# The turn of y in halves of 64 columns, moved behind the state's update

## The chip, the cores and the metric

The kernel runs on one core of a Trainium2 chip. The metric is the time of one execution on the device in microseconds (us); the kernel's figure is the median of several runs. Matrix products run on TensorE (PE; its weight loads are PEld), elementwise work on VectorE (DVE), ScalarE (ACT) and GpSimd (POOL), and SyncE (SP) issues most DMA transfers. Each engine works through its own queue in order; semaphores tie the queues together.

## The reference

Linear attention with a decaying state feeds a layer of eight experts, of which each token uses two. The part that matters here is the attention, with 4 batches, 8 heads, 768 positions and a head width of 64:

```python
for t in range(S):
    state = gamma[None, :, None, None] * state + np.einsum('bhd,bhe->bhde', k[:, :, t], v[:, :, t])
    y[:, :, t] = scale * np.einsum('bhd,bhde->bhe', q[:, :, t], state)
...
x = np.ascontiguousarray(attn_out.transpose(0, 2, 1, 3)).reshape(B * S, H * D)
logits = x @ w_gate
noise_scale = np.log1p(np.exp(x @ w_noise))
noisy_logits = logits + noise_scale * noise
```

The two largest noisy logits of a token choose its experts; each expert is `relu(x @ w1) @ w2`, weighted and added.

## The kernel before, in words

The attention is done in 24 chunks of 128 positions (six per batch; j counts them, c = j % 6). One pass of the loop `for j in range(NCH)` (L822) holds these stages of TensorE:

- **qk(j + 1)** (L353): scores of the next chunk, keys against scaled queries. VectorE masks them into `am` (L356, two instructions).
- **the turn of chunk j - 1**, `x_turn` (L401): y lies as heads by positions and is multiplied, as the stationary operand of 128 columns, with a table `turn` of 144 columns (an identity and the gate's weights), so that it comes out as positions by channels with the logits beside it. Behind it the **squares' sums** (L405): four products of `sq`, the squares of y, with a column of ones.
- **y_state(j)** (L368): queries against the state U that the chunk found (none where c = 0).
- `middle`: products for the lists of tokens that only some chunks have: route_p (L492, L494) in chunks 15 and 23, own_m (L582) in chunk 18.
- **y_mm(j)** (L375): masked scores against scaled values, added to y_state's result. ScalarE copies the result to `yt` (L379).
- **pU(j)** (L384): keys against values, added to the state (none where c = 5). ScalarE copies it to `U` (L386), then squares y into `sq` (L388).

All of a chunk's other work is issued between y_state and y_mm: GpSimd scales values (`v_scale`, L326) and queries (`q_scale`, L334) ahead of time; VectorE computes a token's scale (`x_scale`, L420, L421) from the squares' sums, ScalarE writes the high half of the turned x (x16, L427) and copies the logits (L415), VectorE writes the low half (lo, L431) and SyncE writes both to `xbuf` (L432). `mid` holds VectorE's extra work of single chunks, issued before lo; `todo` stands behind it, and `first_todo` behind y_mm: there ScalarE sums the squares of expert weights (w_sum, L207) and makes their high halves (w_hi, L230). w_hi in chunk 9 needs a scale that a small product (w_scale, L217) yields. The result of the turn, pT, and that of y, pY, have one buffer each, so the next turn waits for lo, and the next y_state for yt.

The order of every queue is the order of the program. The pools decide only how far an engine may run ahead: `vp` has two buffers, `sq` one. From chunk 18 on GpSimd gathers the first expert's tokens, and SyncE transposes them by DMA (`x_t`, L741). Behind the loop TensorE starts on the first expert (L873 to L875) while the last turn and the rest of the lists are done.

Of the kernel before, what the change touches and what calls it, by code (L numbers as in the profile page):

```python
# [20 lines left out]
C = 128  # L21
# [80 lines left out]
def moe_kernel(ctx, tc, qT, kT, kt, vt, noise, wgn, w1, w2, ctab, qtab, xbuf, out):  # L102
# [219 lines left out]

    def v_scale(j):
        c = j % NC
        VP[j] = loads.tile([128, H, D], F32, name="vp", bufs=2)
        nc.gpsimd.tensor_tensor(VP[j], IN["v", j].rearrange("p (h d) -> p h d", h=H),  # L326
                                vtab[:, c, :, None].to_broadcast([128, H, D]), op=OP.mult)

# [18 lines left out]
    def qk(j):  # L347
        AM[j] = loads.tile([128, 2, HP, C], F32, name="am", bufs=2)
        pA = [psum.tile([128, HP, C], F32, name="pA", bufs=2) for _ in range(2)]
        for i in range(HP):  # L350
            for s in range(2):
                r = slice(s * 64, s * 64 + 64)
                nc.tensor.matmul(pA[s][:, i, :], IN["k", j][r, i, :],  # L353
                                 QS[j][r, i, :], start=True, stop=True)
        for s in range(2):
            nc.vector.tensor_tensor(AM[j][:, s], pA[s], mask[:, None, :].to_broadcast([128, HP, C]), op=OP.mult)  # L356
# [5 lines left out]
    def y_state(j):  # L362
        c = j % NC
        PY[j] = loop_psum.tile([128, 2, 512], F32, name="pY")
        for i in range(HP if c else 0):
            for s in range(2):
                r = slice(s * 64, s * 64 + 64)
                nc.tensor.matmul(yplace(j, i, s), U[c % 2][r, i, :], QS[j][r, i, :],  # L368
                                 start=(i < 2), stop=False, skip_group_check=True)

    def y_mm(j):
        c = j % NC
        for i in range(HP):
            for s in range(2):
                nc.tensor.matmul(yplace(j, i, s), VP[j][:, 2 * i + s, :], AM[j][:, s, i, :],  # L375
                                 start=(not c and i < 2), stop=True, skip_group_check=True)
        YT[j] = loads.tile([128, 2, 2, C], F32, name="yt", bufs=2)
        y = YT[j].rearrange("p s g c -> p (s g c)")
        nc.scalar.activation(y.rearrange("p (s x) -> p s x", s=2), PY.pop(j)[:, :, :2 * C], AF.Copy)  # L379
        if c < NC - 1:  # L380
            for i in range(HP):
                for s in range(2):
                    h = 2 * i + s
                    nc.tensor.matmul(pU[s * 64:s * 64 + 64, i, :], IN["kt", j][:, h * 64:h * 64 + 64], VP[j][:, h, :],  # L384
                                     start=(c == 0 and i == 0), stop=True, skip_group_check=True)
            nc.scalar.activation(U[(c + 1) % 2], pU, AF.Copy)  # L386
        SQ[j] = loads.tile([128, KT, C], BF, name="sq", bufs=1)
        nc.scalar.activation(SQ[j].rearrange("p n c -> p (n c)"), y, AF.Square)  # L388

    def x_turn(j):  # L390

        b, c = divmod(j, NC)
        v = int(b >= B0)
        t = loop_psum.tile([128, 2, 512], F32, name="pT").rearrange("p s x -> p (s x)")
        PT[j] = p = t[:, 512 - 2 * XW:512 + 2 * XW]
        p = p.rearrange("p (s x) -> p s x", s=2)
        PT[j, "s"] = t[:, 512 + 2 * XW:513 + 2 * XW]
        y = YT.pop(j)
        for s in range(2):
            for g in range(2):  # L400
                nc.tensor.matmul(p[:, s, g * 128:g * 128 + XW], y[:, s, g, :], turn[:, v, 2 * s + g],  # L401
                                 start=(g == 0), stop=True, skip_group_check=True)
        q = SQ.pop(j)
        for n in range(KT):
            nc.tensor.matmul(PT[j, "s"], q[:, n], oneb[:, 0:1], start=(n == 0), stop=(n == KT - 1), skip_group_check=True)  # L405
        PT[j, "y"] = PT[j].rearrange("p (n x) -> p n x", x=XW)[:, :, :128]
# [343 lines left out]
    def P(j, f, *a, d=mid):  # L750
        d.setdefault(j, []).append((f, a))
# [34 lines left out]
    P(22, route_m, 1)  # L786
    at0(22, route_c, 1)
    P(23, route_p, 1, d=middle)
    P(23, route_n, 1)
    P(23, route_g, 1)  # L790
    at(0, turn_gate, 0)
    at(3, turn_ident, 1)
    at(3, turn_gate, 1)
# [28 lines left out]
    for j in range(NCH):  # L822
        if j + 1 < NCH:
            qk(j + 1)
        if j:
            x_turn(j - 1)
        y_state(j)
        for f, a in middle.get(j, []):
            f(*a)
        if j < 2:  # L830
            q_scale(j + 2)
        if j + 1 < NCH:
            v_scale(j + 1)
        if 2 <= j < NCH - 2:
            q_scale(j + 2)
        if j:
            x_scale(j - 1)
        for f, a in mid.get(j, []):
            f(*a)
        if j < NC - 3:  # L840
            q_table(j + 3)
        if j + AHEAD < NCH:
            load(j + AHEAD)
        if j:
            x_split(j - 1)
        for f, a in todo.get(j, []):
            f(*a)
        y_mm(j)
        for f, a in first_todo.get(j, []):
            f(*a)  # L850
    lctx.close()
# [427 lines left out]
```

## Time and profile before

| | |
|---|---|
| median of 3 runs | 646.7 us (646.54 to 647.61) |
| profiled execution | 645.92 us |
| its span | 644.1 us |
| PE busy | 634.5 us, 99% |
| ACT busy | 300.2 us, 47% |
| DVE busy | 287.6 us, 45% |
| POOL busy | 204.0 us, 32% |

The loop over the chunks ends near 110 us; the experts take the rest. The busy time of PE counts matmuls whose ends are modelled, so stages are best measured from one start to the next. In a row of PE, 128*64 128x128 is the stationary operand (partitions * columns: the tile of the array that is used) and the moving one (partitions x columns); a float32 product makes two records, one for each pass.

### The profile page before, as it was taken

The numbers are of one execution on the slowest core, as the hardware profiler recorded it, in microseconds if no ns is written. First come the engines' busy times: TensorE is split into PE (matmuls) and PEld (weight loads), VectorE is DVE, ScalarE is ACT, GpSimd is POOL, SyncE is SP. The second block draws the span as 40 slices with busy tenths as digits, with TensorE's granted clock in tenths as the row PEclk, the third lists the DMA queues.
The fourth block names the chain that finished last, engine by engine and source line by source line (L and its number), as shares of the span: only waits on it lengthen the run. The fifth ranks groups of instructions, "written<-read, shape, count | busy, mean of one in ns | idle before, by whom it ended". The sixth has DMA issues, their size and how long they took to land.

```text
span 644.1 us, 12255 instructions
## 1 busy us (share of the span) xinstructions
PE 634.5 (99%) x4919; PEld 390.3 (61%) x4919; DVE 287.6 (45%) x740; ACT 300.2 (47%) x559; POOL 204.0 (32%) x166
## 2 busy tenths in 40 slices
PE   9999999999999999999999999999999999999995
PEld 6999998549578544554455445544554465455574
DVE  4678785897454221654162226222622262215020
ACT  6577457615652543554354345434543454344121
POOL 4555472041540134104410433043304430430214
PEclk9999999999999999999999999999999999999999
DMA  8999999978888066845773576447654784483303
GB/s 300 379 386 382 335 319 268 371 188 295 167 139 263 4 130 113 235 99 101 148 191 136 91 137 182 162 82 132 192 161 82 120 211 147 86 118 62 50 10 43
DMA packets 94423, 113.02 MB, mean 175 GB/s; under 512 B 60662, under 2 KB 61820, under 8 KB 90780
## 3 DMA queue, kind: packets, MB, share of 16 engines
q1 hardware_dynamic: 82576, 85.57, 44.2%
q0 software_dynamic: 11776, 26.63, 23.4%
q8 instruction: 40, 0.66, 0.4%
q14 instruction: 19, 0.16, 0.1%
q10 hardware_dynamic: 12, 0.01, 0.0%
HBM read 72.66 MB, written 26.42 MB: 154 GB/s over the span
## 4 chain that ended last, share of the span: by engine, by line
PE 95%; ACT 2%; DVE 1%; issue 1%; POOL 0%; DMA 0%; POOLq 0%; ACTq 0%
PE pH L873 13%; PE pH L875 13%; PE pH L874 13%; PE pO L919 12%; PE pO L921 12%; PE pO L920 12%; PE pA L353 4%; PE pT L401 4%; PE pY L375 4%; PE pT L975 2%; PE pY L368 2%; PE pO L963 2%; PE pU L384 1%; ACT junk L207 1%; PE pO L951 1%; PE pO L949 1%
## 5 line engine op out<-in xcount | busy, mean ns | idle before, releaser
L910 POOL DMA_INDIRECT out<-ot,idx x51 | 82.4, 1616 | 323.2 <-ACT ot L905 181.1
L873 PE MATMUL pH<-xe,w1h 128*128 128x384 f16 (+5 forms) x576 | 180.9, 314 | 0.4 <-DVE hl L882 0.4
L875 PE MATMUL pH<-xe,w1l 128*128 128x384 f16 (+5 forms) x576 | 180.8, 314 | 0.0
L874 PE MATMUL pH<-xe,w1h 128*128 128x384 f16 (+5 forms) x576 | 180.8, 314 | 0.0
L882 DVE SCALAR_TENSOR_TENSOR hl<-pH,hh 128x384 f16<-128x384 f32 (+5 forms) x144 | 75.6, 527 | 140.0 <-ACT hh L879 139.5
L921 PE MATMUL pO<-w2h,hl 128*128 128x512 f16 x344 | 130.4, 379 | 0.0
L920 PE MATMUL pO<-w2l,hh 128*128 128x512 f16 x344 | 130.4, 379 | 0.0
L919 PE MATMUL pO<-w2h,hh 128*128 128x512 f16 x344 | 130.3, 379 | 0.0
L879 ACT ACTIVATE hh<-pH 128x384 f16<-128x384 f32 (+5 forms) x144 | 67.3, 467 | 122.5 <-PE pH L875 111.7
L905 ACT ACTIVATE ot<-pO,gse 128x512 f32<-128x512 f32 x45 | 30.9, 687 | 155.7 <-PE pO L921 139.5
L235 DVE SCALAR_TENSOR_TENSOR w1l<-wst,wsc,w1h 128x1024 f16<-128x1024 f32 x28 | 35.9, 1284 | 95.3 <-ACT w1h L230 95.3
L873 PEld LDWEIGHTS <-w1h 128*128 128x128 f16 x576 | 56.3, 98 | 33.0 <-issue 2.7
L875 PEld LDWEIGHTS <-w1l 128*128 128x128 f16 x576 | 56.3, 98 | 30.9
L874 PEld LDWEIGHTS <-w1h 128*128 128x128 f16 x576 | 56.3, 98 | 30.3 <-issue 0.5
L207 ACT ACTIVATE junk<-wst 128x1024 bf16<-128x1024 f32 x64 | 67.2, 1050 | 0.1
L723 POOL DMA_INDIRECT xg<-xbuf,idx x54 | 57.4, 1062 | 29.0 <-issue 11.9
L921 PEld LDWEIGHTS <-hl 128*128 128x128 f16 x344 | 33.6, 98 | 40.6
L919 PEld LDWEIGHTS <-hh 128*128 128x128 f16 x344 | 33.6, 98 | 40.6 <-issue 0.4
L920 PEld LDWEIGHTS <-hh 128*128 128x128 f16 x344 | 33.6, 98 | 39.6
L356 DVE TENSOR_TENSOR am<-pA,mask 128x512 f32<-128x512 f32 x48 | 30.8, 683 | 17.9 <-PE pA L353 17.9
L326 POOL TENSOR_TENSOR vp<-in_v,cs 128x512 f32<-128x512 f32 x24 | 25.2, 1049 | 36.3 <-issue 16.3
L230 ACT ACTIVATE w2h<-wst,wsc 128x1024 f16<-128x1024 f32 x32 | 36.5, 1140 | 0.2 <-DVE wsc L185 0.2
(181 smaller groups left out, 681.3 us busy)
## 6 DMA issues: line engine op xcount, KB each, us to landing
wst<-w SPq DMA_DIRECT2D x28, 1024.0 KB
in_q<-qT SPq DMA_DIRECT2D x24, 256.0 KB
in_k<-kT SPq DMA_DIRECT2D x24, 256.0 KB
in_v<-vt SPq DMA_DIRECT2D x24, 256.0 KB
in_kt<-kt SPq DMA_DIRECT2D x24, 256.0 KB
xbuf<-x SPq DMA_DIRECT2D x24, 256.0 KB
out<-zero SPq DMA_DIRECT2D x6, 1024.0 KB
wst<-w SPq DMA_DIRECT2D x8, 512.0 KB
```

What stands on the lines that cost most here:

```text
L207: nc.scalar.activation(junk, st[:, i * 1024:(i + 1) * 1024], AF.Square, accum_out=ss[:, i:i + 1])
L230: nc.scalar.activation(hi, st[:, i * 1024:(i + 1) * 1024], AF.Copy, scale=sc[:, 0:1])
L723: nc.gpsimd.indirect_dma_start(out=x[:n], out_offset=None, in_=xbuf[:128 + B0 * S] if e == 0 and t < 3 else xbuf, in_offset=bass.IndirectO ...
L873: nc.tensor.matmul(p[:, :n], whi, xh, start=(k == 0), stop=False)
L874: nc.tensor.matmul(p[:, :n], whi, xl, start=False, stop=False)
L875: nc.tensor.matmul(p[:, :n], wlo, xh, start=False, stop=(k == KT - 1))
L879: nc.scalar.activation(hh[:, f, n0:n1], p, AF.Relu)
L882: nc.vector.scalar_tensor_tensor(hl[:, f, n0:n1], p, 0.0, hh[:, f, n0:n1], op0=OP.max, op1=OP.subtract)
L910: nc.gpsimd.indirect_dma_start(out=out, out_offset=bass.IndirectOffsetOnAxis(ap=idx[:n, i:i + 1], axis=0), in_=ot[:n], in_offset=None, com ...
L919: nc.tensor.matmul(p, a, WT["2h"][:, f, :], start=(f == 0), stop=False)
L920: nc.tensor.matmul(p, a, WT["2l"][:, f, :], start=False, stop=False)
L921: nc.tensor.matmul(p, c, WT["2h"][:, f, :], start=False, stop=(f == FT - 1))
```

## The change

The turn is issued behind y_mm and pU of the chunk, where it stood between qk and y_state. Its four products with 128 stationary columns become eight with 64, each pair writing the two halves of the partitions. y_mm and pU move from the end of the pass to directly behind y_state, ahead of the other engines' work of the pass. `middle` stays behind the turn, and so now stands behind y_mm. `vp` gets a third buffer, `sq` a second. route_n and route_g of the last chunk move from `mid` to `todo`, behind lo.

```diff
-        VP[j] = loads.tile([128, H, D], F32, name="vp", bufs=2)
+        VP[j] = loads.tile([128, H, D], F32, name="vp", bufs=3)
...
-        SQ[j] = loads.tile([128, KT, C], BF, name="sq", bufs=1)
+        SQ[j] = loads.tile([128, KT, C], BF, name="sq", bufs=2)
...
         for s in range(2):
             for g in range(2):
-                nc.tensor.matmul(p[:, s, g * 128:g * 128 + XW], y[:, s, g, :], turn[:, v, 2 * s + g],
-                                 start=(g == 0), stop=True, skip_group_check=True)
+                for r in (slice(0, 64), slice(64, 128)):
+                    nc.tensor.matmul(p[r, s, g * 128:g * 128 + XW], y[:, s, g, r], turn[:, v, 2 * s + g],
+                                     start=(g == 0), stop=True, skip_group_check=True)
...
-    P(23, route_n, 1)
-    P(23, route_g, 1)
+    at(23, route_n, 1)
+    at(23, route_g, 1)
...
         if j + 1 < NCH:
             qk(j + 1)
+        y_state(j)
+        y_mm(j)
         if j:
             x_turn(j - 1)
-        y_state(j)
         for f, a in middle.get(j, []):
...
         for f, a in todo.get(j, []):
             f(*a)
-        y_mm(j)
         for f, a in first_todo.get(j, []):
             f(*a)
```

TensorE's queue in a plain chunk, before, from the end of one turn to the next turn (x8 counts the products; a size is partitions x columns of the result):

```order
L405 MATMUL pT<-oneb,sq 128x1
L368 MATMUL pY<-qs,U_170 64x128 x8
L375 MATMUL pY<-am,vp 64x128 x8
L384 MATMUL pU<-vp,in_kt 64x64 x8
L353 MATMUL pA<-qs,in_k 128x128 x8
L401 MATMUL pT<-turn,yt 128x144 x4
```

The same engine after the change, at a chunk without pU (17), where the new line of the turn is L402 and that of the squares L406:

```order
L406 MATMUL pT<-oneb,sq 128x1
L353 MATMUL pA<-qs,in_k 128x128 x8
L368 MATMUL pY<-qs,U_171 64x128 x8
L375 MATMUL pY<-am,vp 64x128 x8
L402 MATMUL pT<-turn,yt 64x144 x8
L406 LDWEIGHTS sq
```

The turn has moved from behind qk to behind y_mm, and in this chunk nothing stands between the two.

ScalarE's queue around the two w_hi of chunk 9, before (x is x16, lgs the logits, w1h the high half of weights):

```order
L427 ACTIVATE x_926<-pT,xsa 128x512
L415 ACTIVATE lgs_317<-pT 128x32
L379 ACTIVATE yt<-pY 128x512
L386 ACTIVATE U_170<-pU 128x256
L388 ACTIVATE sq<-yt 128x512
L230 ACTIVATE w1h<-wst_474,wsc_476 128x1024 x2
L427 ACTIVATE x_1012<-pT,xsa 128x512
```

And after:

```order
L428 ACTIVATE x_983<-pT,xsa 128x512
L416 ACTIVATE lgs_342<-pT 128x32
L230 ACTIVATE w1h<-wst_507,wsc_509 128x1024 x2
L379 ACTIVATE yt<-pY 128x512
L386 ACTIVATE U_171<-pU 128x256
L388 ACTIVATE sq<-yt 128x512
L428 ACTIVATE x_1073<-pT,xsa 128x512
```

Before, yt and U of chunk 9 stood ahead of the two w_hi; now these stand ahead of yt and U of chunk 10.

## Rows read from the trace of the kernel before

**Rows 1.** Part 4 of the page: chain that ended last, by engine.

```profile
PE 95%; ACT 2%; DVE 1%; issue 1%; POOL 0%; DMA 0%; POOLq 0%; ACTq 0%
```

**Rows 2.** Timeline of PE, one chunk: start us, length us, engine, line, operation, records, [idle before].

```profile
66.43 1.16 PE L353 MATMUL pA<-qs,in_k 64*128 64x128 f32 x16
67.52 1.25 PE L401 MATMUL pT<-turn,yt 128*128 128x144 f32 x8
68.60 0.24 PE L405 MATMUL pT<-oneb,sq 128*128 128x1 bf16 x4
68.78 0.67 PE L368 MATMUL pY<-qs,U 64*64 64x128 f32 x16
69.37 1.09 PE L375 MATMUL pY<-am,vp 128*64 128x128 f32 x16
70.30 0.63 PE L384 MATMUL pU<-vp,in_kt 128*64 128x64 f32 x16
```

**Rows 3.** Timelines of PE cut at stage ends (last records alone), and the last turn.

```profile
70.70 0.23 PE L384 MATMUL pU<-vp,in_kt 128*64 128x64 f32 x2
70.86 0.83 PE L353 MATMUL pA<-qs,in_k 64*128 64x128 f32 x10
...
109.44 0.28 PE L375 MATMUL pY<-am,vp 128*64 128x128 f32 x2
109.65 0.34 PE L873 MATMUL pH<-xe,w1h 128*128 128x384 f16 x1
...
111.61 1.14 PE L401 MATMUL pT<-turn,yt 128*128 128x144 f32 x8
112.59 0.24 PE L405 MATMUL pT<-oneb,sq 128*128 128x1 bf16 x4
```

**Rows 4.** Timelines of PE, DVE and ACT around chunk 9.

```profile
47.39 0.24 PE L405 MATMUL pT<-oneb,sq 128*128 128x1 bf16 x4
...
48.91 0.75 DVE L431 SCALAR_TENSOR_TENSOR x<-pT,xsa,x 128x512 f16<-128x512 f32 x1 [0.89 <-ACT lgs L415]
...
48.10 0.69 ACT L427 ACTIVATE x<-pT,xsa 128x512 f16<-128x512 f32 x1 [0.48 <-DVE xsa L421]
...
50.58 2.18 ACT L230 ACTIVATE w1h<-wst,wsc 128x1024 f16<-128x1024 f32 x2
...
53.85 0.60 ACT L379 ACTIVATE yt<-pY 128x512 f32<-128x512 f32 x1 [0.42 <-PE pY L375]
54.34 0.38 ACT L386 ACTIVATE U<-pU 128x256 f32<-128x256 f32 x1
```

**Rows 5.** Timelines of PE and DVE around chunks 16 and 17.

```profile
78.03 0.24 PE L405 MATMUL pT<-oneb,sq 128*128 128x1 bf16 x4
...
80.28 1.16 PE L353 MATMUL pA<-qs,in_k 64*128 64x128 f32 x16
81.47 1.22 PE L401 MATMUL pT<-turn,yt 128*128 128x144 f32 x8
...
80.58 0.74 DVE L431 SCALAR_TENSOR_TENSOR x<-pT,xsa,x 128x512 f16<-128x512 f32 x1
```

**Rows 6.** Timelines of PE and POOL at chunk 18: own_m and the q scaling behind the gather.

```profile
86.60 0.45 PE L582 MATMUL pR<-ob,a 128*128 128x7 f16 x12
...
90.53 1.27 POOL L334 TENSOR_TENSOR qs<-in_q,gq 128x512 f32<-128x512 f32 x1
```

**Rows 7.** Timelines of PE, SP (issues) and ACT at the loop's end.

```profile
99.50 0.24 PE L405 MATMUL pT<-oneb,sq 128*128 128x1 bf16 x4
...
106.50 1.25 PE L401 MATMUL pT<-turn,yt 128*128 128x144 f32 x8 [0.24 <-ACT yt L379]
...
97.74 0.94 SPq L203 DMA_DIRECT2D wst<-w  x2
...
102.23 2.12 SPq L741 DMA_TRANSPOSE xe<-xg  x1
...
102.86 1.06 ACT L207 ACTIVATE junk<-wst 128x1024 bf16<-128x1024 f32 x1
```

## The prediction

> **What bounds the kernel now.** I read the chain of waits first. TensorE is 95% of the chain that ended last [rows 1], so a change in this loop is worth what it takes off TensorE's own row of work, and costs what it makes TensorE wait. The timeline of one chunk comes next [rows 2]: from one qk to the next are 70.86 - 66.43 = 4.43 us, no row carries an idle mark, and the stages meet end to end. qk takes 1.09 us to the start of the turn, the turn 1.08 to the squares' sums, these 0.18, y_state 0.59, y_mm 0.93 and the pU stage 0.56. So the loop is TensorE-bound in its plain chunks, and its other engines have slack there; the question is where a chunk carries extra work for ScalarE, VectorE or GpSimd, and what that work holds up in the new order.
>
> **The turn itself.** The four products of the turn become eight with half the stationary columns. Two products whose outputs lie in different halves of the partitions run side by side today: eight y_mm products of 64 columns, sixteen passes over 128 moving columns, take 0.93 us [rows 2], and one after the other sixteen passes of the turn's kind would take far more, since eight of them fill the 0.98 us from 111.61 to 112.59 [rows 3]. In y_mm a pair therefore takes 0.93 / 8 = 0.12 us. The turn's moving operand is 144 columns wide, so a pair of half turns should take what one whole pass takes now, 0.98 / 8 = 0.12 us. The halving as such is worth nothing either way; what it does is give the turn the 128*64 shape of y_mm and pU.
>
> **The order of the stages.** A boundary at which the tile's shape changes costs more than a step. From the last pair of pU to the next qk are 70.86 - 70.70 = 0.16 us where a pU step is (70.70 - 70.30) / 7 = 0.06: 0.10 extra. From the last pair of y_mm to a whole-array product are 109.65 - 109.44 = 0.21 us where a step is 0.12: again 0.10 [rows 2, 3]. Entering costs too: the turn of the last chunk, which stands between whole-array products, takes 0.98 us, that of the loop 1.08 [rows 2, 3]. So a chunk of the new order is qk 1.09 (it leaves for another shape, as now) + y_state 0.59 + y_mm 0.93 + pU 0.40 + 0.06 = 0.46 (no change behind it) + turn 0.98 + 0.10 (nothing on entering, 0.10 on leaving) + squares 0.18 = 4.33 us. That is 0.10 less than 4.43. It counts in chunks 1 to 22, so -2.2 us. The bounds are 0 and -0.2 per chunk: no change, or both boundaries of the turn free.
>
> The Trainium skill (TensorEngine Tiling (Array Packing), Key Properties) says that changing the tiling mode, not just the tile, drains TensorE. Rows 3 agree, with some 0.10 us at a change. Counted by that rule alone, both orders have four changes per chunk and the loop gains nothing; the rows say that what is lost on entering also depends on the stage entered. This is a rival below.
>
> **The end of the loop.** In the last chunk the turn of chunk 22 waits 0.24 us for yt [rows 7], because no qk stands before it. In the new order a turn and the squares lie between pU and the next y_state, and y_mm and pU's successor never wait for yt. From pU to the first product of the experts there were five changes of shape (turn, y_state, route_p, y_mm, expert), now three (y_state, y_mm, squares; route_p and the expert follow in the squares' shape). Two changes at 0.10 and the 0.24 make -0.44 us, bounded by -0.24 and -0.7. route_n and route_g now stand behind lo of chunk 22: VectorE work beside TensorE's first expert products, priced at nothing.
>
> **New waits.** GpSimd's and SyncE's queues keep their order. On ScalarE yt, U and sq of a chunk move ahead of x16, of the q tables (chunks 0 to 2; q is scaled more than a chunk before its use, so at nothing) and of what the lists add. The turn stands some 2 us later against qk than before, so what hangs on the turn (x_scale, x16, lo, and what is queued behind them) is late against the next y_state and the next turn. Plain chunks have room. Three places do not; I time each from the start of the squares' sums.
>
> (a) Chunks 9 to 11. ScalarE's two w_hi start 50.58 - 47.39 = 3.19 us after the squares [rows 4]; they wait for a scale whose product now stands directly behind the squares, so 3.0. In the old order yt and U of the chunk stood ahead of them; now yt and U of chunk 10 stand behind. 3.0 + 2.1 for the two and 0.87 from yt's start to U's end (54.34 + 0.38 - 53.85) gives U at 5.97. TensorE wants it for y_state(11) at 0.2 (squares and the scale's product) + 4.33 + 1.09 = 5.6. Wait 0.3. Then x16 of chunk 9 stands behind U and sq: about 6.5, and lo ends 48.91 + 0.75 - 48.10 = 1.56 later, at 8.1. Chunk 11 has no pU, so turn(10) is wanted at 5.9 + 0.59 + 0.93 = 7.45. Wait 0.6. Together +0.9, from 0.3 to 1.3.
>
> (b) Chunk 17 has no pU either. VectorE's list work delays lo of chunk 15, and the turn of 16 starts 81.47 - 78.03 = 3.44 us after the squares [rows 5], 0.15 after lo. It would be ready at 0.18 + 1.09 + 0.59 + 0.93 = 2.79. Wait 0.65, of which today's 81.47 - 80.28 - 1.09 = 0.10 is there already: +0.55, from 0.3 to 0.8.
>
> (c) Chunk 18. own_m now stands behind the squares and directly before qk(20), where y_mm and pU used to follow it. From own_m's start to the end of the q scaling behind the first gather GpSimd needs 90.53 + 1.27 - 86.60 = 5.20 us [rows 6]. qk(21), which reads it, is now wanted after own_m's 0.4 and one chunk, 0.4 + 4.33 = 4.73 after own_m's start. Wait +0.5, from 0 to 0.7. The third vp buffer does not help: the gather stands ahead in GpSimd's queue and waits for own_m's result. The second sq buffer only keeps sq(j) from waiting for the squares of j - 1.
>
> Chunk 3, where VectorE builds the second turn table, is of this kind but not in the sum; it is part of the range's upper side.
>
> (d) SyncE's queue. The last transpose of the first expert's tokens is issued 102.23 - 99.50 = 2.73 us after the squares of chunk 21, behind xbuf's write, which waits for lo. The first expert product stood 109.65 - 102.23 = 7.42 us behind that issue. Now the squares of that turn are followed by 0.18 + 4.33 + (3.39 - 0.44 = 2.95) us of TensorE's work, so 7.46 - 2.73 = 4.73 us are left. Its landing is not shown. The nearest rows: weight pieces issued at 97.74 were read at 102.86, so 5.1 us at most; the transpose's issue alone takes 2.12 us where two weight pieces take 0.94 [rows 7]. I take 5.6, nearest the weight pieces and somewhat above for the longer issue: wait +0.9. The bounds are 2.1 (its issue: no wait) and 7.42 (+2.7).
>
> Sum: -2.2 + 0.9 + 0.55 + 0.5 = -0.25 for the loop, -0.44 + 0.9 = +0.45 for its end, **+0.2 us**. The later stages keep their work; a shift here passes through, TensorE being the chain. The profiled run took 645.92 us (span 644.1), so 646.1 there; against the median of 646.7 it is 646.9.
>
> **Rivals.** *The cover holds* (faster): the engines beside TensorE run far enough ahead at (a) to (c) and the transpose lands in time. Then -2.2 - 0.44 = -2.6, 644.1 us. For it: rows 2 show no idle anywhere. Against: in (a) to (c) the queue orders are fixed and the durations are read. *The transpose lands late* (slower): at 7.42 us after issue the first expert product waits 2.7, the sum is -0.25 - 0.44 + 2.7 = +2.0, 648.7 us; it is slower beyond the bound from a landing of about 6.7 us on. For it: weights and transposes share one queue. Against: nothing waits for it today. *A change of shape costs the same whichever stage is entered* (slower): four per chunk as before, the 2.2 is not there, +2.4, 649.1 us; the skill's rule above read alone. Against: 0.98 and 1.08 for the same turn in rows 2 and 3. *The halves do not run side by side*: 23 turns in the loop and one behind it, eight passes more each, 24 x 0.98 = 23.5, 670 us. Against: y_mm's pairs.
>
> **How the numbers follow.** Forecast 0.56, its own range 645.7 to 648.4; cover holds 0.18; transpose late 0.14; equal cost of changes 0.08; halves in turn 0.04. A measurement of this kernel tells about 0.2%, 1.3 us, from no change. Faster: 0.18 + 0.04 from the forecast's lower end = 0.22. Slower: 0.14 + 0.08 + 0.04 + 0.04 from its upper end = 0.30. Same 0.48. The range 644.9 to 649.1 takes in the forecast, the late transpose, equal changes and the part of the first rival that falls short of its full gain; it leaves out the serial halves and the rest of the first rival, under 0.2.
>
> **What would show it.** In the profile after, a plain chunk of 4.33 us with a turn of 1.08 behind pU shows the step of the shapes; idle before y_state in chunk 11 (released by ScalarE's U), before the turns of 10 and 16 (by VectorE's lo) and before qk(21) (by GpSimd's q scaling) shows (a) to (c); idle before the first expert product, released by a transpose, shows (d). A plain chunk of 4.43 or more, or a turn of 2 us, would make the prediction wrong, and so would a loop without those waits.

## The result

The changed kernel takes 655.04 us (median of 4 runs, 653.75 to 655.19) against 646.62 us: a ratio of 1.0128 [1.0115, 1.0141]. The forecast was 646.9 us with a range of 644.9 to 649.1; the change is slower by 8.4 us and the range misses it by 6. The profiled execution took 653.75 us (span 651.7), 7.8 us more than that of before, so all times of places below add up against 7.8, not 8.4. A ratio in this document is worked out from the runs of both kernels, with its interval, and need not equal the quotient of their medians.

The chain that ended last has lost the single owner that it had in [rows 1]:

```profile
PE 86%; DVE 5%; DMA 4%; ACT 2%; issue 1%; SPq 1%; POOL 0%; POOLq 0%; ACTq 0%; DVEq 0%
```

A plain chunk of the changed kernel, in the timeline of PE (start us, length us, engine, line, operation, records, [idle before]), beside [rows 2]:

```profile
69.11 1.16 PE L353 MATMUL pA<-qs,in_k 64*128 64x128 f32 x16
...
71.72 0.64 PE L384 MATMUL pU<-vp,in_kt 128*64 128x64 f32 x16
72.18 1.15 PE L402 MATMUL pT<-turn,yt 128*64 128x144 f32 x16
73.27 0.25 PE L406 MATMUL pT<-oneb,sq 128*128 128x1 bf16 x4
73.45 0.71 PE L353 MATMUL pA<-qs,in_k 64*128 64x128 f32 x8
```

From qk to qk are 73.45 - 69.11 = 4.34 us, against 4.43 in [rows 2]; pU takes 0.46 and the turn 1.09. That part came as forecast (4.33). What did not are the waits of PE, which the timeline marks in brackets with what ended them:

```profile
58.52 1.20 PE L402 MATMUL pT<-turn,yt 128*64 128x144 f32 x16 [0.66 <-DVE x L432]
...
63.45 1.20 PE L402 MATMUL pT<-turn,yt 128*64 128x144 f32 x16 [0.96 <-DVE x L432]
...
85.98 1.20 PE L402 MATMUL pT<-turn,yt 128*64 128x144 f32 x16 [0.49 <-DVE cum L547]
...
96.76 1.71 PE L353 MATMUL pA<-qs,in_k 64*128 64x128 f32 x16 [0.95 <-POOL qs L334]
...
101.40 1.20 PE L402 MATMUL pT<-turn,yt 128*64 128x144 f32 x16 [0.85 <-DVE x L432]
...
113.26 0.67 PE L368 MATMUL pY<-qs,U 64*64 64x128 f32 x16 [1.79 <-ACT U L386]
...
116.74 0.32 PE L874 MATMUL pH<-xe,w1h 128*128 128x384 f16 x1
116.91 0.32 PE L875 MATMUL pH<-xe,w1h 128*128 128x384 f16 x1
```

The first expert product starts at 116.74 us instead of 109.65 [rows 3]: 7.1 of the 7.8 us are lost by then. (The last turn, now of half tiles between whole-array products, takes 0.35 more; the rest passes through.) I measured each stage against its length in a plain chunk and got these losses:

| place | us more | forecast |
|---|---|---|
| first stages, before any turn | 0.75 | 0 |
| qk(6) behind chunk 3's tables | 0.73 | named, not priced |
| small: chunks 8 and 9 (0.2), y_state(11) (0.16) | 0.4 | 0.3 for y_state(11) |
| turn(10), turn(11) | 0.85 + 1.15 | 0.6 for turn(10) |
| turn(16) | 0.7, of which 0.1 before the change | 0.55 |
| qk(21) | 1.57 | 0.5 |
| turn(19) | 1.05 | 0 |
| y_state(23), turn(22) | 1.86 + 0.58 | 0 |
| first expert product, for the transposes | 0 | 0.9 |

Together 9.6 us, against some 2.5 us gained by the shapes and at the loop's end. The first line is not the change's: the second pass starts at 10.80 before and 11.55 here, but over the profiles of all kernels below it lies anywhere between 10.67 and 11.55, with no regard to the edit.

**What VectorE did there.** In the timelines of DVE and POOL of the changed kernel (two halves of w1l on one row are "x2"):

```profile
55.29 2.42 DVE L242 SCALAR_TENSOR_TENSOR w1l<-wst,wsc,w1h 128x512 f16<-128x512 f32 x2
...
93.10 2.95 DVE L443 TENSOR_TENSOR lg<-lgs 128x96 f32<-128x96 f32 x1
95.98 1.28 DVE L356 TENSOR_TENSOR am<-pA,mask 128x512 f32<-128x512 f32 x2
...
97.42 3.17 DVE L242 SCALAR_TENSOR_TENSOR w1l<-wst,wsc,w1h 128x512 f16<-128x512 f32 x2
```

```profile
92.48 1.15 POOL L724 DMA_INDIRECT xg<-xbuf,idx  x1 [5.09 <-DVE idx L637]
93.66 1.05 POOL L326 TENSOR_TENSOR vp<-in_v,cs 128x512 f32<-128x512 f32 x1
94.67 1.26 POOL L334 TENSOR_TENSOR qs<-in_q,gq 128x512 f32<-128x512 f32 x1
...
97.09 1.05 POOL L326 TENSOR_TENSOR vp<-in_v,cs 128x512 f32<-128x512 f32 x1
98.09 1.27 POOL L334 TENSOR_TENSOR qs<-in_q,gq 128x512 f32<-128x512 f32 x1
```

The sum of 96 columns at 93.10 ends at 96.05, right when GpSimd's two scalings do (95.93). So the masks start at 95.98 and end their first half 0.68 us later, at 96.66, and qk(21), which writes where they read, starts at 96.76. The row names GpSimd's q scaling for this wait, but that had ended 0.8 us earlier: it was the masks.

One thing about this sum stays open. It starts 0.56 us before the first scaling, beside a gather (92.48), and so should have been over by 93.35. In the kernel before, the same sum as far behind the start of a gather (88.06) took its usual time:

```profile
88.68 0.25 DVE L442 TENSOR_TENSOR lg<-lgs 128x96 f32<-128x96 f32 x1
```

There the scaling followed only at 89.53. That the sum ends with the scalings is shown; why it stood still ahead of them is not.

Over the loop (groups of instructions: busy us, mean ns), first before, then after the change:

```profile
L242 DVE SCALAR_TENSOR_TENSOR w1l<-wst,wsc,w1h 128x512 f16<-128x512 f32 x8 | 6.0, 796 | 0.0
L442 DVE TENSOR_TENSOR lg<-lgs 128x96 f32<-128x96 f32 x4 | 1.9, 466 | 0.1
L356 DVE TENSOR_TENSOR am<-pA,mask 128x512 f32<-128x512 f32 x48 | 30.8, 683 | 17.9 <-PE pA L353 17.9
L431 DVE SCALAR_TENSOR_TENSOR x<-pT,xsa,x 128x512 f16<-128x512 f32 x24 | 17.9, 747 | 7.0 <-ACT lgs L415 6.9
```

```profile
L242 DVE SCALAR_TENSOR_TENSOR w1l<-wst,wsc,w1h 128x512 f16<-128x512 f32 x8 | 9.4, 1219 | 0.0
L443 DVE TENSOR_TENSOR lg<-lgs 128x96 f32<-128x96 f32 x3 | 4.5, 1497 | 0.0
L356 DVE TENSOR_TENSOR am<-pA,mask 128x512 f32<-128x512 f32 x48 | 30.5, 677 | 4.9 <-PE pA L353 4.9
L432 DVE SCALAR_TENSOR_TENSOR x<-pT,xsa,x 128x512 f16<-128x512 f32 x22 | 16.4, 746 | 10.4 <-ACT lgs L416 10.3
```

In the mean the low halves (L242) became 1.5 times and the sums 3.2 times as long; both read only SBUF, the on-chip memory of the engines. The masks and lo, which read a result of TensorE, did not. The Trainium skill (SBUF — State Buffer, SBUF: two separate sides) says that a VectorE instruction with two inputs in SBUF and a GpSimd instruction that reads SBUF take turns on one pair of ports, and that the one that starts first holds it for its whole instruction while the other is blocked. The trace agrees on who is held up and who is not; it differs on how long, since the half at 97.42 took 2.50 us and stood still over the end of one scaling (98.14) and all of the next.

### The profile page after: what moved, and what is told of

Its sections match the earlier page's. It is cut to its first block, busy times and chain, and to the rows that moved or that the text cites. A ratio compares the mean times of both kernels' runs of the same rounds, so it can differ in the third digit from the quotient of the medians.

```text
span 651.7 us, 12651 instructions
## 1 busy us (share of the span) xinstructions
PE 635.9 (98%) x5111; PEld 387.2 (59%) x5111; DVE 294.3 (45%) x740; ACT 299.0 (46%) x559; POOL 204.8 (31%) x166
## 4 chain that ended last, share of the span: by engine, by line
PE 86%; DVE 5%; DMA 4%; ACT 2%; issue 1%; SPq 1%; POOL 0%; POOLq 0%; ACTq 0%; DVEq 0%
PE pH L874 13%; PE pH L876 13%; PE pH L875 13%; PE pO L920 11%; PE pO L921 11%; PE pO L922 11%; PE pA L353 2%; PE pT L402 2%; PE pT L976 2%; DMA wst<-w 2%; PE pY L375 2%; PE pO L964 2%; DVE x L432 1%; DVE w1l L242 1%; ACT junk L207 1%
## 5 line engine op out<-in xcount | busy, mean ns | idle before, releaser
L911 POOL DMA_INDIRECT out<-ot,idx x51 | 83.8, 1644 | 315.9 <-ACT ot L906 190.9
L724 POOL DMA_INDIRECT xg<-xbuf,idx x54 | 55.6, 1029 | 40.5 <-issue 12.2
L334 POOL TENSOR_TENSOR qs<-in_q,gq 128x512 f32<-128x512 f32 (+1 forms) x24 | 30.2, 1258 | 33.0 <-DMA in_q<-qT 20.7
L230 ACT ACTIVATE w1h<-wst,wsc 128x1024 f16<-128x1024 f32 x32 | 36.1, 1138 | 1.3 <-DVE wsc L185 1.3
```

The source lines that it names most:

```text
L230: nc.scalar.activation(hi, st[:, i * 1024:(i + 1) * 1024], AF.Copy, scale=sc[:, 0:1])
L724: nc.gpsimd.indirect_dma_start(out=x[:n], out_offset=None, in_=xbuf[:128 + B0 * S] if e == 0 and t < 3 else xbuf, in_offset=bass.IndirectO ...
L911: nc.gpsimd.indirect_dma_start(out=out, out_offset=bass.IndirectOffsetOnAxis(ap=idx[:n, i:i + 1], axis=0), in_=ot[:n], in_offset=None, com ...
```

## The experiments

Three theories stood against each other. **Order**: the moved stages turn the one-off work of VectorE, ScalarE and SyncE into waits of TensorE. **Contention**: GpSimd's scalings now lie beside VectorE's list work and hold it up. **Shape**: the half tiles cost by themselves.

### The halves, apart from the place

The turn in halves where it stood before:

```diff
-                nc.tensor.matmul(p[:, s, g * 128:g * 128 + XW], y[:, s, g, :], turn[:, v, 2 * s + g],
+                for r in (slice(0, 64), slice(64, 128)):
+                    nc.tensor.matmul(p[r, s, g * 128:g * 128 + XW], y[:, s, g, r], turn[:, v, 2 * s + g],
...
```

> The kernel before with only the turn's halves of 64 columns; its place between qk and y_state and all buffers stay. Every queue beside TensorE keeps its order, so whatever differs is the shape. If halves run side by side and a change of shape costs 0.10 us (the step of the prediction), there is one change more per chunk, in front of the squares: 646.6 + 23 x 0.10 = 648.9 us, turn 1.08 as before. If entering the squares costs nothing, 646.6. If the halving itself is what made the change slow, 653 or more, and a chunk of 4.7 us.

648.49 us, 1.0036 [1.0016, 1.0056]. The timeline of PE:

```profile
68.35 1.20 PE L402 MATMUL pT<-turn,yt 128*64 128x144 f32 x16
69.48 0.25 PE L406 MATMUL pT<-oneb,sq 128*128 128x1 bf16 x4
69.67 0.67 PE L368 MATMUL pY<-qs,U 64*64 64x128 f32 x16
```

The turn takes 1.13 us instead of 1.08, turn and squares 1.32 instead of 1.26 [rows 2]: 0.06 per chunk. Shape as the cause of 8 us falls.

The counterpart, the changed kernel with the four products of 128 columns:

```diff
-                for r in (slice(0, 64), slice(64, 128)):
-                    nc.tensor.matmul(p[r, s, g * 128:g * 128 + XW], y[:, s, g, r], turn[:, v, 2 * s + g],
+                nc.tensor.matmul(p[:, s, g * 128:g * 128 + XW], y[:, s, g, :], turn[:, v, 2 * s + g],
...
```

> The changed kernel with the four products of 128 columns in the turn, in its new place. If the prediction's step of the shapes is right, the turn now changes shape against pU and no more against the squares: pU 0.56 and turn 1.0 to 1.08 against 0.46 and 1.09, so a plain chunk of 4.35 to 4.44 and at most 0.1 us x 22 = 2.2 us slower than the changed kernel, where waits don't take it up: 655 to 657. If the halves bring nothing, 655.0 and a chunk of 4.35.

656.85 us, 1.0169 [1.0147, 1.0191]; the plain chunk is 4.43 us again:

```profile
51.03 1.16 PE L353 MATMUL pA<-qs,in_k 64*128 64x128 f32 x16
...
55.46 0.76 PE L353 MATMUL pA<-qs,in_k 64*128 64x128 f32 x7
```

Place alone gives nothing, halves alone cost 0.06; only both together give 0.09 per chunk. The step of the shapes holds.

### The third vp buffer in the old order

```diff
-        VP[j] = loads.tile([128, H, D], F32, name="vp", bufs=2)
+        VP[j] = loads.tile([128, H, D], F32, name="vp", bufs=3)
```

> The kernel before with a third vp buffer alone. GpSimd's value scaling no longer waits for pU (11.9 us in 7 waits before), so its work moves in the pass while the order of all queues stays. Contention theory: VectorE's list work may now fall beside GpSimd's and TensorE may wait, 646.4 to 649; order theory: 646.4 within 0.5.

655.0 us, 1.0128 [1.0111, 1.0145]: one buffer more, with every queue in its old order, costs as much as the whole change, and far more than either theory expected. TensorE waits before five turns, 7.7 us in all, four times for lo and once for list work. (The profiled run took 656.42 us.) Why shows in the timelines of POOL and DVE near 57 us. In the kernel before, the value scaling waits for pU (its buffer is read there), and the pair is over at 56.69, just before the list work begins:

```profile
54.41 1.04 POOL L326 TENSOR_TENSOR vp<-in_v,cs 128x512 f32<-128x512 f32 x1 [2.26 <-PE pU L384]
55.41 1.28 POOL L334 TENSOR_TENSOR qs<-in_q,gq 128x512 f32<-128x512 f32 x1
...
56.91 1.40 DVE L242 SCALAR_TENSOR_TENSOR w1l<-wst,wsc,w1h 128x512 f16<-128x512 f32 x2
```

With three buffers that tie is gone, the values are scaled early, and the q scaling waits for something else and lies on the list work:

```profile
57.02 1.27 POOL L334 TENSOR_TENSOR qs<-in_q,gq 128x512 f32<-128x512 f32 x1 [1.21 <-PE pT L405]
...
57.31 3.01 DVE L242 SCALAR_TENSOR_TENSOR w1l<-wst,wsc,w1h 128x512 f16<-128x512 f32 x2
...
101.92 1.95 PE L401 MATMUL pT<-turn,yt 128*128 128x144 f32 x8 [2.92 <-DVE x L431]
```

To be sure that it is this and not the buffers' place, the same kernel with GpSimd's scalings in four instructions each:

```diff
-    eng, m = nc.vector if j == 0 else nc.gpsimd, 2 if j < 2 else 1
+    eng, m = nc.vector if j == 0 else nc.gpsimd, 2 if j < 2 else 4
...
+        for x in range(0, H, 2):
+            nc.gpsimd.tensor_tensor(VP[j][:, x:x + 2], IN["v", j].rearrange("p (h d) -> p h d", h=H)[:, x:x + 2],
+                                    vtab[:, c, x:x + 2, None].to_broadcast([128, 2, D]), op=OP.mult)
```

> The kernel before with the third vp buffer (which alone made it 655.0 us) and GpSimd's scalings in four instructions of 128 columns. Contention theory: the 8.5 us of the third buffer are VectorE instructions that stand still while GpSimd's two follow each other (0.25 us becomes 2.96, 0.74 becomes 2.50), and TensorE waits of 1.85 and 2.92 us for lo behind them; short GpSimd instructions let VectorE in between, so most of it goes: 647 to 650 us. If the third buffer costs by something else (the place of the buffers, the loads), 654 or more.

648.9 us, 1.004 [1.0028, 1.0051]: 6 of the 8.5 us are back, and the low halves take 852 ns in the mean, where they take 1290 with the scalings whole:

```profile
L242 DVE SCALAR_TENSOR_TENSOR w1l<-wst,wsc,w1h 128x512 f16<-128x512 f32 x8 | 6.5, 852 | 0.0
```

The sums take 0.25 us again too. That is no proof that VectorE gets in between two parts: the sum at 90.28 is over before GpSimd's first part starts at 90.84.

The plainest form of the theory is work on GpSimd that nobody waits for, in the old kernel:

```diff
+        if 3 <= j < 18:
+            nc.gpsimd.tensor_tensor(idle, gq[:, 0], gq[:, 0], op=OP.mult)
```

> The kernel before, with one product on GpSimd more in each of passes 3 to 17: a 128x512 tensor_tensor of the q table with itself into a tile that nothing reads, behind q_scale. It takes 1.3 us of the 2 us that GpSimd is idle in a pass, reads and writes only its own memory, and no engine waits for it. Contention theory: VectorE's instructions between tiles in SBUF (the low halves of weights at L242, the sums at L442, the table at L311) stand still while GpSimd computes, so those that fall beside the extra product take 1.3 to 2.5 us instead of 0.25 to 0.74, lo and the masks come late, and TensorE waits in chunks 3, 9 to 12 and 16: 648 to 651 us. Order theory (only the order of the queues makes the waits): nothing waits for the product, at most 0.5 us: 646.4 to 646.9.

648.38 us, 1.0033 [1.0019, 1.0047]. It took 1.04 us an instruction. In its timelines the half of w1l beside it is longer, lo behind it late, and TensorE waits at 64.23 for a result that has nothing to do with GpSimd:

```profile
56.82 1.05 POOL L838 TENSOR_TENSOR idle<-gq 128x512 f32<-128x512 f32 x1
...
57.14 1.93 DVE L242 SCALAR_TENSOR_TENSOR w1l<-wst,wsc,w1h 128x512 f16<-128x512 f32 x2
...
64.23 1.22 PE L402 MATMUL pT<-turn,yt 128*128 128x144 f32 x8 [0.47 <-DVE x L432]
```

Contention is shown as a cause, in the old order, three times.

### How much of it is in the changed kernel

Two vp buffers again, in the new order:

```diff
-        VP[j] = loads.tile([128, H, D], F32, name="vp", bufs=3)
+        VP[j] = loads.tile([128, H, D], F32, name="vp", bufs=2)
```

> The changed kernel with two vp buffers, as before, instead of three. Contention theory: the third buffer frees GpSimd's value scaling from waiting for pU and lets it fall beside VectorE's list work, whose instructions it stretches; with two buffers the VectorE instructions at 56, 61, 93 and 97 us shrink to under 1.2 us and the time falls by 2 us or more, to 653 or less. Order theory: the waits are set by the order of the queues, 654.5 to 655.7 us. Against both: with two buffers GpSimd waits for a pU that now ends earlier in the pass, so its own times may hardly move, 655.0.

653.84 us, 1.0114 [1.0078, 1.015]: not told apart from the changed kernel, and L242 still takes 1.77 and 2.50 us. The tie to pU does not place GpSimd's work there any more: the q scaling at 60.00, beside the half of 1.77 us, waited 1.24 us for the load of its query, and the pair beside a sum of 2.96 us (93.14) starts at 93.70, directly behind a gather. So the third buffer, which alone makes the old order slow, is not what makes the new order slow.

GpSimd's scalings in four parts, the edit shown above, in the changed kernel:

> The changed kernel with GpSimd's scalings of q and v in four instructions of 128 columns each instead of one of 512. If VectorE's instruction waits for the GpSimd instruction under way to end, its longest stretch falls from 1.0 - 2.7 us to about 0.3 us, and the waits before the turns of 10, 11 and 19 and in chunk 3 mostly go: 652 to 653.5 us. If GpSimd keeps the memory for itself over instructions that follow each other closely, the stretches stay at 1 to 2.7 us and the time at 654.5 to 656. Four starts instead of one may cost GpSimd 0.1 to 0.3 us per chunk, which only qk(21) would feel.

651.91 us, 1.0083 [1.0066, 1.01], 3.1 us better. VectorE's low halves take 916 ns in the mean instead of 1219, its sums 246 (here too the sum beside a gather is over, at 93.97, before the first part starts, at 94.28). GpSimd pays more than was expected: a part of 128 columns of q takes 492 ns in the mean, four of them 1.97 us instead of 1.31.

No scalings at all:

```diff
-                                  bufs=AHEAD + {"k": 0, "q": -1, "v": 0, "kt": 1}[n])
+                                  bufs=AHEAD + {"k": 0, "q": 1, "v": 1, "kt": 1}[n])
...
-        VP[j] = loads.tile([128, H, D], F32, name="vp", bufs=3)
-        nc.gpsimd.tensor_tensor(VP[j], IN["v", j].rearrange("p (h d) -> p h d", h=H),
-                                vtab[:, c, :, None].to_broadcast([128, H, D]), op=OP.mult)
+        VP[j] = IN["v", j].rearrange("p (h d) -> p h d", h=H)
...
-        QS[j] = loads.tile([128, HP, C], F32, name="qs", bufs=3)
+        if j > 1:
+            QS[j] = IN["q", j]
+            return
+        QS[j] = loads.tile([128, HP, C], F32, name="qs", bufs=2)
```

The products read q and v as loaded, so their tiles are held longer and get two and one more buffers.

> The changed kernel without GpSimd's scalings of q and v: the products read q and v as loaded (so the values and the experts' lists are other ones, and the part behind the loop is not to be compared; the measure is the start of the first expert product, 109.65 us before and 116.9 after the change). GpSimd then computes nothing beside VectorE's list work, and no qk waits for it. Contention theory: chunk 3, the turns of 10, 11 and 19 and qk(21) with its masks wait no more (0.73 + 0.83 + 1.14 + 1.03 + 1.56 = 5.3 us), the turn of 16, y_state(23) and turn(22) still do: 111.6 us, up to 0.6 less if the first stages take 0.83 instead of 1.39. Order theory (VectorE's and ScalarE's one-off work is too long for its new place even without GpSimd): only qk(21)'s own wait goes, 115 to 116.

The first expert product starts at 113.14 us, 3.6 earlier than in the changed kernel; contention theory said 111 to 111.6, order theory 115 to 116. L242 takes 742 ns throughout, and at qk(6), turn(11), turn(19) and qk(21) the waits are gone or 0.1. Left are these waits of PE (us in total, times, longest), which are order theory's:

```profile
PE pY L369 <- ACT U L387: 1.5, 2, 0.9
PE pT L403 <- DVE x L433: 0.7, 2, 0.4
...
PE pT L403 <- DVE cum L548: 0.5, 1, 0.5
```

Chunk 19 lost 1.9 us of its own there, in steps between single products of pU and the turn; what it waited for the trace does not show, and I leave it open. Without it the time would be within the contention theory's. Its first stages were 0.6 us shorter, so of the 9.6 us some 3.0 (3.6 - 0.6) to 4.9 (with the 1.9) go with GpSimd's scalings and what they wait for; the rest, without the 0.75 at the start, I put down to the order.

An attempt to put GpSimd's pair back beside lo and the masks, by a tie to y_state:

```diff
-        QS[j] = loads.tile([128, HP, C], F32, name="qs", bufs=3)
+        QS[j] = loads.tile([128, HP, C], F32, name="qs", bufs=2)
...
+        if 2 <= j < NCH - 2:
+            q_scale(j + 2)
         if j + 1 < NCH:
             v_scale(j + 1)
-        if 2 <= j < NCH - 2:
-            q_scale(j + 2)
```

> The changed kernel with two qs buffers instead of three and GpSimd's q scaling ahead of its v scaling in the pass. The first then waits for y_state of the pass, which reads the buffer that it overwrites, so GpSimd's two instructions lie from 1.7 to 4.0 us behind the start of qk, beside VectorE's lo and masks (which read PSUM and were never stretched) instead of beside its list work. Contention theory (what counts is at which time of the pass GpSimd computes): the stretches at 27, 56, 61, 74 and 97 us go, and with them the waits of chunk 3 (0.73), of the turns of 10 and 11 (0.66 and 0.96) and of 19 (0.85); qk(21) no longer waits for a v scaling in front of its q: 650 to 651.5 us. Order theory: 654.5 or more, since the q scaling now starts later and qk may wait for it.

654.2 us, 1.0108 [1.0082, 1.0134]: contention's 650 to 651.5 is missed, and order's 654.5 lies nearer. Qk(21) and turn(19) lost their waits. But at 60.40 the q scaling waited 1.65 us for the load of its query, not for y_state, a low half there and list work at 84 us took 1.79 and 2.18 us, and U for y_state(23) came later, behind a load of w2 for which ScalarE waited 4.85 us. (The profiled run took 657.64 us.) One tie does not keep two engines apart here.

### The order's own part

The loads of w2 two passes earlier:

```diff
-        at((20, 20, 21, 21)[i], w_load, 0, "2", i)
+        at((18, 18, 19, 19)[i], w_load, 0, "2", i)
```

> The changed kernel with the four loads of the second weight (w2) issued in passes 18, 18, 19, 19 instead of 20, 20, 21, 21. Order theory: in the changed kernel ScalarE's sum of squares (w_sum) waits 2.9 us for such a load and stands ahead of yt and U of chunk 22, so y_state(23) waits 1.79 us and turn(22) another 0.37; with the data there in time both go: 655.0 - 1.8 to 2.2 = 652.8 to 653.2 us. Rival: U is late by ScalarE's work itself or the loads are slow for lack of bandwidth wherever they are issued: 654.5 to 655.5, and y_state(23) still waits over 1 us.

653.11 us, 1.0103 [1.0073, 1.0134]. The wait of y_state(23) is gone, as forecast; turn(22) still waits, 0.55 us. The gain of 1.9 lies at the edge of what the intervals tell, and the profile shows less: the first expert product starts 1.6 us earlier (115.10), but 0.8 of it is the second pass, which starts at 10.75. Elsewhere in the loop qk waits 2.2 us for q scalings instead of 0.9. In the changed kernel ScalarE's timeline had shown it:

```profile
111.30 1.06 ACT L207 ACTIVATE junk<-wst 128x1024 bf16<-128x1024 f32 x1 [2.93 <-DMA wst<-w]
...
112.83 0.37 ACT L386 ACTIVATE U<-pU 128x256 f32<-128x256 f32 x1
```

The sum of squares of a weight that lands late now stands ahead of yt and U; before, it stood behind them.

VectorE's extra work behind lo instead of ahead of it:

```diff
         if j:
             x_split(j - 1)
+        for f, a in late.get(j, []):
+            f(*a)
...
-    P(14, route_m, 0)
+    L(14, route_m, 0)
...
-        P(j, w_lo_half, 0, "1", i)
+        L(j, w_lo_half, 0, "1", i)
```

> The changed kernel with VectorE's extra list work and low halves of weights (mid) issued behind lo of the same pass instead of ahead of it (own_s and slots, which the gather needs, stay). Order theory: the turns of 10, 11, 16 and 19 wait 0.66 + 0.96 + 0.49 + 0.85 = 2.96 us for lo or for what lo waits for, because this work stands ahead of it; the waits go: 655.0 - 2.5 to 3.0 = 652.0 to 652.5 us. Contention theory: these VectorE instructions take 1.8 to 3.0 us where they take 0.25 to 0.74 alone, because GpSimd's scalings run beside them, wherever they stand; they then delay the masks and the waits come back at qk or y_mm: 654.3 or more.

662.72 us, 1.0259 [1.0224, 1.0293], 8 us slower. Order's 652.0 to 652.5 is wrong; contention's "654.3 or more", with the waits back at qk, holds, but nothing in it said how much more. VectorE waits for ScalarE's x16 before it can write lo (0.89 in [rows 4]), 20 times here and 19.6 us in all, where the changed kernel has 10 such waits and 10.3 us: the extra work used to fill that gap. Behind lo it stands before the masks, which then hold up qk:

```profile
66.52 2.43 DVE L242 SCALAR_TENSOR_TENSOR w1l<-wst,wsc,w1h 128x512 f16<-128x512 f32 x2
...
69.88 1.28 DVE L356 TENSOR_TENSOR am<-pA,mask 128x512 f32<-128x512 f32 x2
...
70.66 1.60 PE L353 MATMUL pA<-qs,in_k 64*128 64x128 f32 x15 [1.50 <-POOL vp L326]
```

The writes of x one pass later, since SyncE waits 20.5 us for lo in front of them and the loads stand behind:

```diff
-        nc.sync.dma_start(xbuf[128 + j * C:128 + (j + 1) * C, :DM], x.rearrange("p a d -> p (a d)").bitcast(F32))
+        held.append((j, x))
+        while len(held) > (1 if j < NCH - 1 else 0):
+            i, x = held.pop(0)
+            nc.sync.dma_start(xbuf[128 + i * C:128 + (i + 1) * C, :DM], x.rearrange("p a d -> p (a d)").bitcast(F32))
```

> The changed kernel with each write of x to xbuf issued one pass later (x16 gets a fourth buffer for it). In the changed kernel SyncE waits 20.5 us for lo in front of these writes (7.3 before), and the loads of the next chunks stand behind them; the DMA engines, full at 380 to 390 GB/s in the kernel before, move 315 to 331 GB/s from 20 to 35 us, and GpSimd waits 20.7 us for queries (6.6 before). Loads theory: SyncE's waits for lo go, 380 GB/s come back, GpSimd waits under 8 us for queries, its work leaves VectorE's list work, and part of the waits of TensorE go: 651.5 to 653.5 us. Order theory: the waits for lo and qs are set by the queues of VectorE and GpSimd alone, 654.3 to 655.5.

653.92 us, 1.0127 [1.0104, 1.0151]: no gain that can be told. SyncE's wait for lo fell to 9.4 us and the DMA engines moved 363 and 383 GB/s from 25 to 35 us instead of 323 and 331, but GpSimd still waited 21.7 us for queries. So the writes are not why the queries come late, and the loads theory falls as far as it rests on them; what late queries cost in the new order (20.7 us of GpSimd's waits instead of 6.6) stays open.

### Mixtures

The tie, the early w2, the second table in passes 5 and 8, the last turn whole (the first two as above):

```diff
-    at(3, turn_ident, 1)
-    at(3, turn_gate, 1)
+    at(5, turn_ident, 1)
+    at(8, turn_gate, 1)
...
+                for r in (slice(0, 64), slice(64, 128)) if j < NCH - 1 else (slice(0, 128),):
```

> As the run before it, with the w2 loads two passes earlier, the second turn table built in passes 5 and 8 instead of both parts in pass 3, and the last turn (which lies between the experts' products) with 128 columns again. If the losses add up as the contention and order theories together say, these take 1.9, up to 0.7 and 0.3 us off the run before: 647.0 to 649.0 us. If it came to 644.5, all of the shapes' gain of some 2.4 us would be there.

The tie, four parts, w2 one pass earlier, tables and list work spread behind lo, the last turn whole:

```diff
-    P(16, own_h, 0, 0, 7)
+    at(16, own_h, 0, 0, 7)
...
-    P(17, own_h, 0, 7, 12)
-    P(17, own_t, 0)
+    at(17, own_h, 0, 7, 12)
+    at(17, own_t, 0)
...
-        P(j, w_lo_half, 0, "1", i)
+        (P if i in (0, 1, 3, 5) else at)(j, w_lo_half, 0, "1", i)
```

> The changed kernel with what helped so far together: GpSimd's scalings in four parts, q ahead of v behind y_state; the w2 loads one pass earlier; the second turn table in passes 2 to 4, one piece each; own_h, own_t and the second low half of each of passes 10 to 12 behind lo; the last turn with 128 columns. By the sums so far 655.0 - 3.1 (parts) - 1.9 (w2) - 0.3 (last turn) - up to 2.5 (turns of 10 and 16, chunk 3) = 647 to 650 us; the transposes of the first expert's tokens, which are late by some 4 us against the kernel before because the lists are one turn later, keep it above 646. Under 645.2 it would be faster than the kernel before.

The two best edits and the last turn whole:

```diff
-        at((20, 20, 21, 21)[i], w_load, 0, "2", i)
+        at((19, 19, 20, 20)[i], w_load, 0, "2", i)
```

> The changed kernel with the two edits that helped most, GpSimd's scalings in four parts and the w2 loads one pass earlier, and the last turn with 128 columns. If their gains add: 655.0 - 3.1 - 1.9 - 0.3 = 649.7 us, 649 to 651. If the transposes of the first expert's tokens are what is late next, as in the two mixed kernels: 651 to 653, with a wait of the first expert product for a transpose.

They took 651.39 us, 1.0091 [1.0058, 1.0123]; 656.0 us, 1.0124 [1.0086, 1.0162]; and 653.83 us, 1.0093 [1.0058, 1.0128] (single runs from 650.37 to 658.99). None beats the kernel before, and none reaches what was expected of it if the gains added; of the last the other expectation, 651 to 653 with a wait for a transpose, comes nearest. In each the loop's waits shrank, and what came next was the forecast's (d): the first expert product waited 1.8, 3.2 and 6.9 us for a transpose. The last, whose profiled run took 658.99 us, with rows of PE and one stretch (busy us of PE, PEld, DVE, ACT, POOL, granted clock, DMA share, GB/s):

```profile
120.31 0.48 PE L875 MATMUL pH<-xe,w1h 128*128 128x384 f16 x1 [6.95 <-DMA xe<-xg]
120.58 0.52 PE L876 MATMUL pH<-xe,w1h 128*128 128x384 f16 x1
120.90 0.52 PE L877 MATMUL pH<-xe,w1l 128*128 128x384 f16 x1
```

```profile
122.00:124.00 2.00, 2.00 (x8) 0.96 (x7) 0.00 (x0) 0.00 (x0) 0.00 (x0) 0.50 1.05 409
```

The wait costs twice: behind it the granted clock is 0.50, the lower of its two levels (1.2 GHz), and a product takes 0.32 us from one start to the next, where the changed kernel takes 0.17 (116.74 to 116.91).

## Why the prediction was wrong

- **The shapes: right.** 4.33 forecast, 4.34 measured, halves side by side at 1.09 us. The rival of equal costs and that of serial halves fall. The loop gained some 2.0 of its 2.2 (22 chunks at 0.09).
- **The step that failed: "the durations are read".** This stands in the prediction against *the cover holds*, and (a) to (c) rest on it: all durations, and with them how long VectorE's other work stands in the way, were taken from the kernel before as fixed. They are not. A low half takes 0.74 us and a sum 0.25 where GpSimd is quiet, and up to 2.50 and 2.95 beside its scalings. So waits that stood in the sum came out larger, and places that the sum had at nothing waited too. Without the scalings 3.0 to 4.9 of the 9.6 us are gone.
- **(a): the mechanism right, the size wrong.** The forecast's path, the two w_hi ahead of U and x16, shows alone in the kernel without scalings: marked waits of 0.57 for y_state(11) and 0.37 for turn(10), 0.9 in all, as forecast. In the changed kernel 2.4 instead of 1.4 us of low halves stand ahead of lo as well: 2.0 at turn(10) and turn(11) instead of 0.6 at turn(10).
- **(c) and turn(19): the size wrong, and the release.** The sign that was named, idle before qk(21) marked with GpSimd's q scaling, is there, but the release was the masks behind a 2.95 us sum: 1.57 instead of 0.5. Turn(19) waits behind the next low halves (3.17 us for two): 1.05, where the sum had nothing.
- **(b): right**, 0.6 above what was there before for 0.55, and the same marked wait of 0.49 without scalings: it is the length of VectorE's own list work.
- **Chunk 3**: named but left out of the sum; 0.73, gone in the kernel without scalings.
- **The end of the loop: a term was missing.** The wait of 0.24 for yt is gone, and "y_mm and pU's successor never wait for yt" held. But y_state(23) also needs U, and the step did not look there: ScalarE's sum of w2 squares in the new order stands ahead of yt and U of chunk 22 and itself waits for a load. The load was read 5.3 us after its issue (105.99), much as before (5.1); what changed is what stands behind the sum. It cost 1.86, and 0.58 at the next turn. [Rows 7] held both ends of it (loads issued at 97.74, the sum at 102.86), and I used them only for the transposes.
- **"The third vp buffer does not help": wrong for the old order.** I asked what it could bring and priced it at nothing; alone, in the old order, it costs some 8.5 us. Freeing an engine from a wait moved its work onto another's. In the new order its price is not told from nothing (653.84 without it), so it does not explain the 8.4 us by itself: the rows of that run have the two engines' work side by side all the same.
- **(d): right in kind, hidden here.** TensorE was later than the transposes (0 for 0.9). When the other waits were cut, it was what ended last, at 1.8 to 6.9 us. (The squares at 99.50 are those of chunk 20, in pass 21; the count of what follows them is not changed by that.)
- **The range** was made from orders and fixed durations. No rival said that an instruction's duration could change by where another engine's work lies, so no bound could reach 655.

The cause is shown in kind: contention by the buffer, the parts and the idle product in the old order and by the missing scalings in the new one, the late U by the earlier loads. How the 8.4 us divide is only bounded, since no kernel here gets them back.

## What to carry to other kernels

Before a move or an added buffer, lay the SBUF-to-SBUF work of VectorE and GpSimd side by side in the timeline: a wait that keeps them apart (in the old order a value scaling waiting for its buffer) is worth something, though it looks like idle time. Price a buffer by where the freed engine's work goes, not by the wait that it removes. A duration read from a trace holds only beside the neighbours that it had there; where two engines can hold each other up, bound it by the longest such row.

## What was not expected of the hardware

- A sum of 96 columns that takes 0.25 us took 2.95, and a low half of 512 columns 2.50 for 0.74: the half got in only when a run of two GpSimd instructions had ended, not just the one under way; the sum too ended with such a run. With four short GpSimd instructions for each long one the low halves took 916 ns in the mean instead of 1219, and GpSimd's scaling of q 1.97 us instead of 1.31.
- After a wait of 2.92 us (the third vp buffer) the turn took 1.95 us instead of 1.22, with the granted clock at 0.50 in the stretch behind it (below); the longest wait of the changed kernel, 1.79 us, left it at 1.00. But in the kernel with the extra work behind lo a shorter one, 1.50 us (70.66), was followed by 0.56 from 72 to 74 us, and y_mm took 1.76 us instead of 0.93.

```profile
103.00:104.00 1.00, 1.00 (x12) 0.90 (x15) 0.00 (x1) 0.00 (x0) 0.00 (x0) 0.50 0.80 286
```
